# The last token group's closing sums: other banks, another order, one queue for the first output's stores

## The chip, the cores and the metric

The kernel runs on one NeuronCore of a Trainium2 chip. Its engines have queues of their own: TensorE (matmuls, and transposes by a matmul with the identity), VectorE and ScalarE (elementwise work, and the only ones that read what TensorE wrote to PSUM), GpSimd, and SyncE, which here only issues DMAs. ScalarE issues DMAs too. An engine takes its instructions in order; between engines, semaphores order the work. The metric is the device time of one execution in microseconds.

## The reference

A state-space block gives 3072 tokens of 256 features; they go through an expansion to 2048 features with a parametric ReLU, and back to 256. The change touches the end of the second product.

```
attn_out = _attn_ref(x, a, B, C)                  # (4, 8, 768, 32), scan in chunks
x = attn_out.transpose(0, 2, 1, 3).reshape(3072, 256)
h = x @ w_in                                      # (3072, 2048)
g = np.maximum(h, 0.0) + alpha * np.minimum(h, 0.0)
return (g @ w_out).astype(np.float32)             # (3072, 256)
```

## The kernel before

The tokens are worked on in six groups of 512 (`g`), the last being `g == NG - 1`. In each but the first, the 2048 hidden features are taken in four steps (`z`, called quads) of four blocks of 128. Both matrix products use a seven-product scheme in place of eight: the token half and the feature half of each operand are split in two, sums of them are formed on GpSimd and VectorE, and seven products are accumulated in PSUM. For the second product, `product(g, z, n)` (L1085) adds the share of quad `z` to sum number `n`. It is called for quad `z - 1` among the work of quad `z`, so that only the last quad's seven products are left for the end, in `close` (L1218).

A PSUM bank holds 512 numbers per partition, so two sums of 256 columns share one. `HALVES` and `LAST` (L1079, L1081) say for each sum the bank and the half of it; four banks are used, the fourth (`m5_bank`) for sum 5 and, in the last group, sum 4. In the last group sum 3 is computed turned, with tokens on the partitions, in two halves of 128 tokens (L1092 to L1100): its halves lie side by side in one half of bank 2. Before, sums 7 and 6 share bank 1. The framework tracks a bank as one tile: a matmul into it waits for an earlier read of any of its columns, and a read waits for the matmuls into it that were recorded before it.

`close` turns the seven sums into four 128 x 256 blocks of the output and stores them:

- `c[0][:, 0]` = sums 1 + 2, the first output. It is transposed in 32 x 32 blocks on VectorE in `turn` (L1276) and stored with four DMAs of 32 KB, in turn on SyncE and ScalarE.
- `c[0][:, 1]` = 6 + 1 + 5, to which 3 is added at the end. TensorE transposes it (`turned`, L1226), ScalarE copies it from PSUM to `rest`, and VectorE adds the halves of sum 3 to it (L1273). Each half has a store of its own.
- `c[1][:, 1]` = 7 + u + 5 and `c[1][:, 0]` = 7 + u - 4, where `u[:, 0]` = 6 + 1 and `u[:, 1]` = 7 + `u[:, 0]`. Both are transposed by TensorE, copied by ScalarE and stored with one 128 KB DMA each (`send`, L1232).

Just before `close`, `finish` stores the second output block of the group before (512 tokens, four DMAs of 64 KB on SyncE), so that these stores stand ahead of those of `close` in SyncE's queue. The order within each engine is the order of the calls in the source. Output buffers come from a pool of three (`op`).

Of the kernel before, what the change touches and what calls it, by code (L numbers as in the profile page):

```python
# [9 lines left out]
F32 = mybir.dt.float32  # L10
U32 = mybir.dt.uint32
U16 = mybir.dt.uint16
ALU = mybir.AluOpType
# [9 lines left out]
def kernel(  # L23
# [25 lines left out]
    nc = tc.nc  # L49
# [6 lines left out]
    P = 128  # L56
# [15 lines left out]
    NQ = NF // 2  # L72
    NZ = NF // 4
    HM = d_model // 2
    HT = GT // 2
# [13 lines left out]
    wtp = ctx.enter_context(tc.tile_pool(name="wtp", bufs=3))  # L89
# [8 lines left out]
    op = ctx.enter_context(tc.tile_pool(name="op", bufs=3))  # L98
    dr = ctx.enter_context(tc.tile_pool(name="dr", bufs=1, space=bass.MemoryType.DRAM))
    ps_s = ctx.enter_context(tc.tile_pool(name="ps_s", bufs=2, space=PSUM))  # L100
# [3 lines left out]
    def bank(i):  # L104


        return ps_q.tile([P, 512], F32, name="bank", tag=f"q{i}")
# [215 lines left out]
    def keep_warm(to, n, cols=2 * Q):  # L323

        for i in range(n):
# [8 lines left out]
                          in_=ident.unsqueeze(1).to_broadcast([P, H, Q]))  # L334
# [182 lines left out]
    def spare():  # L517

        return ps_h.tile([P, GT], F32, name="hp", tag="hp")
# [483 lines left out]
    def hidden_two(g, f, t0, hp):  # L1003


        nt = GT // 2
        ts = slice(t0, t0 + nt)
        for i in range(2):
            fs = slice((f + i) * P, (f + i + 1) * P)
            for k in range(KC):  # L1010
                nc.tensor.matmul(hp[:, i * nt : (i + 1) * nt], w_in[:, k, fs],  # L1011
                                 xts[g][:, k, ts], start=(i == 0 and k == 0),
                                 stop=(k == KC - 1), skip_group_check=True)
        for i in range(2):
            if t0 == 0:
                gts[g, f + i] = gp.tile([P, GT], F32, name="gt")
            nc.scalar.mul(gts[g, f + i][:, ts], hp[:, i * nt : (i + 1) * nt],
                          s_alpha[:, f + i : f + i + 1])

        def rest():  # L1020
            for i in range(2):
                gt = gts[g, f + i][:, ts]
                nc.vector.scalar_tensor_tensor(
                    out=gt, in0=hp[:, i * nt : (i + 1) * nt], scalar=s_mul[:, f + i : f + i + 1],
                    in1=gt, op0=ALU.mult, op1=ALU.max)
        return rest
# [51 lines left out]
    ms = {}  # L1078
    HALVES = {1: (0, 0), 2: (0, 1), 7: (1, 0), 6: (1, 1), 3: (2, 0), 4: (2, 1), 5: (3, 0)}  # L1079

    LAST = {**HALVES, 4: (3, 1)}  # L1081
    blocks = {}


    def product(g, z, n, parts=(0, 1), halves=(0, 1)):  # L1085

        if g not in ms:
            ms[g] = [t.rearrange("p (h t) -> p h t", h=2)
                     for t in [bank(i) for i in range(3)] + m5_bank]
        i, h = (LAST if g == NG - 1 else HALVES)[n]  # L1090
        s1, s2, s4 = out_sums
        if g == NG - 1 and n == 3:  # L1092
            for s in halves:
                ts = slice(s * P, (s + 1) * P)
                for p in parts:
                    q = 2 * z + p
                    nc.tensor.matmul(ms[g][i][:, h, ts], blocks[g, z][n][:, p, ts], s4[:, q],  # L1097
                                     start=(q == 0 and h == 0 and s == 0), stop=(q == NQ - 1),
                                     skip_group_check=True)
            return  # L1100
        for p in parts:
            q = 2 * z + p
            w = {1: wq[:, q, 0, 0], 2: wq[:, q, 1, 0], 3: s4[:, q], 4: wq[:, q, 1, 1],
                 5: s1[:, q], 6: s2[:, q], 7: wq[:, q, 0, 1]}[n]
            nc.tensor.matmul(ms[g][i][:, h], w, blocks[g, z][n][:, p],  # L1105
                             start=(q == 0 and h == 0), stop=(q == NQ - 1),
                             skip_group_check=True)
# [110 lines left out]
    def close(g):  # L1218

        m = {n: ms[g][i][:, h] for n, (i, h) in LAST.items()}  # L1220
        sa = wtp.tile([P, 2, HT], F32, name="sa", tag="wr")
        u = wtp.tile([P, 2, HT], F32, name="u", tag="wr")
        c = [one.tile([P, 2, HT], F32, name=f"c{i}") for i in range(2)]
        add = nc.vector.tensor_tensor

        def turned(t, ps):  # L1226

            for b in range(2):
                nc.tensor.transpose(ps[:, b * P : (b + 1) * P], t[:, b * P : (b + 1) * P], ident)
            return ps  # L1230

        def send(i, h, o, dma, bs=(0, 1)):  # L1232

            t0, n = g * GT + h * HT + bs[0] * P, len(bs)
            dma.dma_start(out=out[t0 : t0 + n * P, i * HM : (i + 1) * HM]
                          .rearrange("(b p) m -> p b m", p=P),
                          in_=o[:, bs[0] : bs[0] + n])

        def tokens():
            return op.tile([P, 2, HM], F32, name="o_sb")  # L1240

        for n in (1, 2):
            product(g, NZ - 1, n)
        nc.scalar.copy(out=sa[:, 0], in_=m[1])
        add(out=c[0][:, 0], in0=m[2], in1=sa[:, 0], op=ALU.add)
        turn(g, 0, c[0], slice(0, HT), [nc.sync, nc.scalar])
        product(g, NZ - 1, 6)
        add(out=u[:, 0], in0=m[6], in1=sa[:, 0], op=ALU.add)  # L1248
        product(g, NZ - 1, 5)
        nc.scalar.copy(out=sa[:, 1], in_=m[5])  # L1250
        add(out=c[0][:, 1], in0=u[:, 0], in1=sa[:, 1], op=ALU.add)
        product(g, NZ - 1, 7)
        add(out=u[:, 1], in0=m[7], in1=u[:, 0], op=ALU.add)
        add(out=c[1][:, 1], in0=u[:, 1], in1=sa[:, 1], op=ALU.add)
        ps = [ps_h.tile([P, 512], F32, name="turned", tag="hp") for i in range(2)]
        turned(c[0][:, 1], ps[0])
        rest = tokens()
        nc.scalar.copy(out=rest.rearrange("p b m -> p (b m)"), in_=ps[0][:, :HT])
        product(g, NZ - 1, 4)
        add(out=c[1][:, 0], in0=u[:, 1], in1=m[4], op=ALU.subtract)  # L1260
        turned(c[1][:, 1], ps[1])
        o = tokens()
        nc.scalar.copy(out=o.rearrange("p b m -> p (b m)"), in_=ps[1][:, :HT])
        send(1, 1, o, nc.sync)
        product(g, NZ - 1, 3, halves=(0,))
        ps = ps_s.tile([P, 512], F32, name="turned", tag="ss")
        turned(c[1][:, 0], ps)
        o = tokens()
        nc.scalar.copy(out=o.rearrange("p b m -> p (b m)"), in_=ps[:, :HT])
        send(1, 0, o, nc.scalar)  # L1270
        product(g, NZ - 1, 3, halves=(1,))
        for b in range(2):
            add(out=rest[:, b], in0=m[3][:, b * P : (b + 1) * P], in1=rest[:, b], op=ALU.add)  # L1273
            send(0, 1, rest, (nc.sync, nc.scalar)[b], (b,))

    def turn(g, i, c, ts, engs):  # L1276

        n = ts.stop - ts.start
        o = op.tile([P, GT], F32, name="o_sb")
        nc.vector.transpose(o[:, :n], c.rearrange("p h t -> p (h t)")[:, ts])  # L1280
        for a4 in range(P // 32):
            m0 = i * HM + 32 * a4
            t0 = g * GT + ts.start
            engs[a4 % len(engs)].dma_start(
                out=out[t0 : t0 + n, m0 : m0 + 32].rearrange("(b r) c -> r b c", r=32),
                in_=o[32 * a4 : 32 * a4 + 32, :n].rearrange("r (b c) -> r b c", c=32))
# [44 lines left out]
    rest = hidden_two(0, 2, 2 * Q, spare())  # L1331
# [61 lines left out]
    for i in range(NZ * (NG - 1)):  # L1393
        g, z = divmod(NZ + i, NZ)
# [39 lines left out]
        if i == 0:  # L1434
            load_pair(nxt + 1)
        quad(g, z, after, nxt >= NP or z % 2 == 0)
    close(NG - 1)


# [28 lines left out]
```

## Time and profile before

| What | us |
|---|---|
| median of four runs (lowest, highest) | 359.28 (359.07, 359.45) |
| the profiled execution: its time | 359.07 |
| its span, from first to last instruction | 357.4 |
| TensorE busy from 0 to 340 | 336.64 |
| TensorE busy from 340 to 350 | 9.83 |
| TensorE busy from 350 to the end | 3.57 |
| last matmul of the kernel starts | 353.66 |
| last store issued (ScalarE) | 354.55 |

The granted clock of TensorE is 1.0 throughout. The table's middle rows are from the busy time of each engine by stretches; the last two are single instructions of the trace.

A page or an answer of the trace is read like this: a row of the order of time gives the start, the length, the engine (PE is TensorE, PEld its weight loads, DVE VectorE, ACT ScalarE, POOL GpSimd, SP SyncE; a q behind the name stands for the sequencer that issues DMAs), the line of the kernel, the operation, the tile that is written and the tiles that are read, the size, and in brackets the idle time of that engine before it and what ended it. Each fp32 matmul of the source appears as two in the trace. Ends of matmuls are modelled, since they overlap.

### The profile page before, as it was taken

The page shows a single profiled execution, that of the slowest core. Times are in us where ns is not written, and L with a number is a line of the kernel's source. Part 1 is how long each engine was busy: PE and PEld are TensorE (multiplying, and loading weights), DVE is VectorE, ACT ScalarE, POOL GpSimd, SP SyncE. Part 2 cuts the span into 40 slices and gives each one's busy share as a digit, 9 for nine tenths or more (in the row PEclk, how much of TensorE's full clock was granted, in tenths as well). Part 3 has the DMA queues.
Part 4 walks back from the last instruction along what each step waited for, and adds up shares of the span by engine and source line. Part 5 has one row for each costly group of instructions (what it writes and reads, how often), then busy time and mean ns, then how long its engine had stood idle before and what let it go on. Part 6 is the DMA issues. An engine that isn't in the chain of part 4 may idle for free.

```text
span 357.4 us, 7565 instructions
## 1 busy us (share of the span) xinstructions
PE 350.0 (98%) x2894; PEld 287.6 (80%) x2894; DVE 240.4 (67%) x467; ACT 174.1 (49%) x387; POOL 205.6 (58%) x221
## 2 busy tenths in 40 slices
PE   8899999999999999999999999999999999999995
PEld 7576665578788888888888888888888888888884
DVE  7988986998748756857747847757856633653263
ACT  3677666535356346346345445345445344444331
POOL 4887568589939755725645725647626535533520
PEclk9999999999999999999999999999999999999999
DMA  7999999608245403403503413413001002002004
GB/s 112 195 188 324 292 224 234 137 17 181 84 91 125 95 2 76 103 2 85 99 26 79 89 45 74 88 48 73 2 4 29 0 2 31 0 0 32 0 3 88
DMA packets 105469, 30.19 MB, mean 84 GB/s; under 512 B 79880, under 2 KB 101336, under 8 KB 105432
## 3 DMA queue, kind: packets, MB, share of 16 engines
q1 hardware_dynamic: 104360, 29.39, 37.6%
q8 instruction: 23, 0.38, 0.4%
q10 hardware_dynamic: 1072, 0.31, 0.4%
q14 instruction: 14, 0.11, 0.1%
HBM read 26.32 MB, written 3.37 MB: 83 GB/s over the span
## 4 chain that ended last, share of the span: by engine, by line
PE 94%; POOL 1%; DMA 1%; ACT 1%; SPq 1%; issue 1%; DVE 1%; ACTq 0%; DVEq 0%; POOLq 0%
PE bank L1105 33%; PE hp L1130 28%; PE bank L1034 8%; PE hp L996 6%; PE ss L1130 6%; PE hp L1011 2%; PE ss L758 1%; PE ss L702 1%; PE bank L1097 1%; PE ss L750 1%; DMA nat<-in_C_dram 1%; PE ss L776 1%; PE ss L713 1%; PE bank L511 1%; PE ss L589 1%
## 5 line engine op out<-in xcount | busy, mean ns | idle before, releaser
L1187 POOL TENSOR_TENSOR gt<-gt 128x512 f32<-128x512 f32 x58 | 74.3, 1281 | 21.1 <-DVE gt L1115 16.2
L1105 PE MATMUL bank<-gt,w_out 128*128 128x256 f32 x320 | 83.8, 382 | 0.2 <-DVE u L1248 0.2
L1105 PEld LDWEIGHTS bank<-gt,w_out 128*128 128x128 f32 x320 | 60.0, 190 | 9.7 <-issue 1.6
L1115 DVE SCALAR_TENSOR_TENSOR gt<-hp,s_mul,gt 128x256 f32<-128x256 f32 x96 | 42.0, 479 | 29.1 <-ACT gt L1113 26.8
L1177 POOL TENSOR_TENSOR gt<-gt 128x512 f32<-128x512 f32 x20 | 25.4, 1271 | 62.5 <-DVE gt L1115 56.7
L1113 ACT ACTIVATE gt<-hp,s_alpha 128x256 f32<-128x256 f32 x96 | 40.4, 472 | 34.5 <-PE hp L1130 31.4
L1105 PE MATMUL bank<-gt,ws 128*128 128x256 f32 x224 | 55.9, 379 | 0.0
L1105 PEld LDWEIGHTS bank<-gt,ws 128*128 128x128 f32 x224 | 42.3, 190 | 5.6
L1130 PE MATMUL hp<-xs,w_in 128*128 128x256 f32 x160 | 41.9, 384 | 0.0
L1130 PE MATMUL hp<-xs,ws 128*128 128x256 f32 x160 | 41.2, 380 | 0.0
L1156 DVE TENSOR_TENSOR hp<-hp,u 128x512 f32<-128x512 f32 x20 | 14.0, 700 | 35.8 <-ACT u L1154 35.8
L1130 PEld LDWEIGHTS hp<-xs,ws 128*128 128x128 f32 x160 | 30.3, 190 | 4.3 <-POOL xs L1075 0.2
L1130 PEld LDWEIGHTS hp<-xs,w_in 128*128 128x128 f32 x160 | 29.7, 190 | 4.5
L1034 PE MATMUL bank<-w_out,gt 128*128 128x256 f32 x128 | 31.0, 384 | 0.0
L1034 PEld LDWEIGHTS bank<-w_out,gt 128*128 128x128 f32 x128 | 23.6, 190 | 6.5 <-issue 2.9
L1130 PE MATMUL ss<-xT,w_in 128*128 128x256 f32 x96 | 24.6, 379 | 0.0
L996 PE MATMUL hp<-xT,w_in 128*128 128x512 f32 x48 | 22.7, 596 | 0.1
L616 POOL TENSOR_TENSOR sm<-state,bmask 128x256 f32<-128x256 f32 (+1 forms) x10 | 6.2, 621 | 28.8 <-DVE state L613 28.8
L532 DVE TENSOR_TENSOR_SCAN dec<-abc,bank 128x192 f32<-128x192 f32 x48 | 22.7, 521 | 0.0
L1145 ACT COPY m<-hp 128x512 f32<-128x512 f32 x8 | 4.7, 587 | 35.7 <-PE hp L1130 35.7
L1154 ACT COPY u<-hp 128x512 f32<-128x512 f32 x20 | 11.7, 586 | 19.4 <-PE hp L1130 19.4
L1115 DVE SCALAR_TENSOR_TENSOR gt<-c,s_mul,gt 128x256 f32<-128x256 f32 x40 | 20.6, 555 | 0.0
(204 smaller groups left out, 617.3 us busy)
## 6 DMA issues: line engine op xcount, KB each, us to landing
abc<-z SPq DMA_DIRECT2D x24, 192.0 KB
raw<-in_moe_w_in_dram SPq DMA_DIRECT2D x8, 512.0 KB
raw<-in_moe_w_out_dram SPq DMA_DIRECT2D x8, 512.0 KB
abc<-z SPq DMA_DIRECT2D x8, 512.0 KB
out_dram<-o_sb SPq DMA_DIRECT2D x33, 64.0 KB
nat<-in_B_dram SPq DMA_DIRECT2D x26, 64.0 KB
nat<-in_C_dram SPq DMA_DIRECT2D x24, 64.0 KB
xt<-in_x_dram SPq DMA_DIRECT2D x12, 128.0 KB
```

What stands on the lines that cost most here:

```text
L532: nc.vector.tensor_tensor_scan(out=dv[:, o : o + SQ], data0=abc[k][:, s : s + SQ], data1=ident_p[0][:, :SQ], initial=0.0, op0=ALU.mult, op ...
L996: nc.tensor.matmul(hp, w_in[:, k, f * P : (f + 1) * P], xts[g][:, k], start=(k == 0), stop=(k == KC - 1))
L1011: nc.tensor.matmul(hp[:, i * nt : (i + 1) * nt], w_in[:, k, fs], xts[g][:, k, ts], start=(i == 0 and k == 0), stop=(k == KC - 1), skip_gro ...
L1034: nc.tensor.matmul(pos[0][t // 2][:, t % 2], gt[:, t * Q : (t + 1) * Q], w_out[:, f], start=(f == 0 and t % 2 == 0), stop=(f == NF - 1), s ...
L1105: nc.tensor.matmul(ms[g][i][:, h], w, blocks[g, z][n][:, p], start=(q == 0 and h == 0), stop=(q == NQ - 1), skip_group_check=True)
L1113: nc.scalar.mul(o[:, p], h[:, p], s_alpha[:, fs[p]])
L1115: nc.vector.scalar_tensor_tensor(out=o[:, p], in0=h[:, p], scalar=s_mul[:, fs[p]], in1=o[:, p], op0=ALU.mult, op1=ALU.max)
L1130: nc.tensor.matmul(to[:, p], w(2 * z + p), b, start=start and p == 0, stop=True, skip_group_check=True)
L1154: nc.scalar.copy(out=u2, in_=A)
L1156: nc.vector.tensor_tensor(out=Y, in0=Y, in1=u2, op=ALU.add)
L1177: nc.gpsimd.tensor_tensor(out=tc_, in0=g22, in1=g12, op=ALU.subtract)
L1187: eng.tensor_tensor(out=o, in0=x0, in1=x1, op=ALU.subtract)
```

## The change

Three things change, all in `product` and `close` for the last group:

- **Banks.** Sum 7 moves to the second half of bank 2. The two halves of sum 3 no longer lie side by side: the first is in the first half of bank 2 (128 columns), the second in the first half of bank 1 (`third_of`), where sum 7 was. So bank 1 holds sum 6 and the second half of sum 3, bank 2 sum 7 and the first half of sum 3.
- **Order.** TensorE takes the last quad's products as 1, 2, 6, 5, 7, 4, the transposes of `c[0][:, 1]`, the first half of 3, the transposes of `c[1][:, 1]` and of `c[1][:, 0]`, the second half of 3. Before, it was 1, 2, 6, 5, 7, the transposes of `c[0][:, 1]`, 4, those of `c[1][:, 1]`, the first half of 3, those of `c[1][:, 0]`, the second half. VectorE forms `u[:, 0]` ahead of the transpose of the first output, not behind it, and adds the first half of sum 3 on its own.
- **Stores.** All four stores of the first output are issued by SyncE (two by ScalarE before). Both halves of `rest` go out from SyncE too (the second from ScalarE before), the first of them now ahead of `c[1][:, 1]`. `c[1][:, 0]` stays on ScalarE. `rest` comes from another pool (`wtp`).

```diff
-    LAST = {**HALVES, 4: (3, 1)}
+    LAST = {**HALVES, 4: (3, 1), 7: (2, 1)}
+    def third_of(g, s):
+        return ms[g][2 - s][:, 0, :P]
...
-                    nc.tensor.matmul(ms[g][i][:, h, ts], blocks[g, z][n][:, p, ts], s4[:, q],
-                                     start=(q == 0 and h == 0 and s == 0), stop=(q == NQ - 1),
-                                     skip_group_check=True)
+                    nc.tensor.matmul(third_of(g, s), blocks[g, z][n][:, p, ts], s4[:, q],
+                                     start=q == 0, stop=(q == NQ - 1), skip_group_check=True)
...
+        def by_act(t, ps, o=None):
+            turned(t, ps)
+            o = tokens() if o is None else o
+            nc.scalar.copy(out=o.rearrange("p b m -> p (b m)"), in_=ps[:, :HT])
+            return o
...
-        turn(g, 0, c[0], slice(0, HT), [nc.sync, nc.scalar])
-        product(g, NZ - 1, 6)
+        for n in (6, 5):
+            product(g, NZ - 1, n)
         add(out=u[:, 0], in0=m[6], in1=sa[:, 0], op=ALU.add)
-        product(g, NZ - 1, 5)
         nc.scalar.copy(out=sa[:, 1], in_=m[5])
+        turn(g, 0, c[0], slice(0, HT), [nc.sync])
+        product(g, NZ - 1, 7)
         add(out=c[0][:, 1], in0=u[:, 0], in1=sa[:, 1], op=ALU.add)
-        product(g, NZ - 1, 7)
         add(out=u[:, 1], in0=m[7], in1=u[:, 0], op=ALU.add)
+        product(g, NZ - 1, 4)
         add(out=c[1][:, 1], in0=u[:, 1], in1=sa[:, 1], op=ALU.add)
+        add(out=c[1][:, 0], in0=u[:, 1], in1=m[4], op=ALU.subtract)
         ps = [ps_h.tile([P, 512], F32, name="turned", tag="hp") for i in range(2)]
-        turned(c[0][:, 1], ps[0])
-        rest = tokens()
-        nc.scalar.copy(out=rest.rearrange("p b m -> p (b m)"), in_=ps[0][:, :HT])
-        product(g, NZ - 1, 4)
-        add(out=c[1][:, 0], in0=u[:, 1], in1=m[4], op=ALU.subtract)
-        turned(c[1][:, 1], ps[1])
-        o = tokens()
-        nc.scalar.copy(out=o.rearrange("p b m -> p (b m)"), in_=ps[1][:, :HT])
-        send(1, 1, o, nc.sync)
+        rest = wtp.tile([P, 2, HT], F32, name="rest", tag="wt")[:, 0]
+        rest = by_act(c[0][:, 1], ps[0], rest.rearrange("p (b m) -> p b m", b=2))
         product(g, NZ - 1, 3, halves=(0,))
-        ps = ps_s.tile([P, 512], F32, name="turned", tag="ss")
-        turned(c[1][:, 0], ps)
-        o = tokens()
-        nc.scalar.copy(out=o.rearrange("p b m -> p (b m)"), in_=ps[:, :HT])
+        add(out=rest[:, 0], in0=third_of(g, 0), in1=rest[:, 0], op=ALU.add)
+        send(0, 1, rest, nc.sync, (0,))
+        send(1, 1, by_act(c[1][:, 1], ps[1]), nc.sync)
+        o = by_act(c[1][:, 0], ps_s.tile([P, 512], F32, name="turned", tag="ss"))
+        product(g, NZ - 1, 3, halves=(1,))
+        add(out=rest[:, 1], in0=third_of(g, 1), in1=rest[:, 1], op=ALU.add)
         send(1, 0, o, nc.scalar)
-        product(g, NZ - 1, 3, halves=(1,))
-        for b in range(2):
-            add(out=rest[:, b], in0=m[3][:, b * P : (b + 1) * P], in1=rest[:, b], op=ALU.add)
-            send(0, 1, rest, (nc.sync, nc.scalar)[b], (b,))
+        send(0, 1, rest, nc.sync, (1,))
```

## The prediction

> **What bounds it now.** First the page: busy shares and the chain say whether one engine carries the span. Then the order of time over the last ten microseconds, since only the close of the last token group is edited; then that stretch's waits and transfers.
>
> ```profile
> span 357.4 us, 7565 instructions
> ...
> PE 350.0 (98%) x2894; PEld 287.6 (80%) x2894; DVE 240.4 (67%) x467; ACT 174.1 (49%) x387; POOL 205.6 (58%) x221
> ...
> PE 94%; POOL 1%; DMA 1%; ACT 1%; SPq 1%; issue 1%; DVE 1%; ACTq 0%; DVEq 0%; POOLq 0%
> ```
>
> TensorE is the bound for 347 us, and nothing there changes in amount: the built order shows the same matmuls before and after. What can change is the close, where TensorE waits. Columns: start, length (merged where several), engine, line, what, and in brackets the idle time before and its releaser.
>
> ```profile
> 348.86 0.45 DVE L1280 STREAM_TRANSPOSE o_sb<-c 128x256 f32<-128x256 f32 x1
> 349.23 0.38 DVE L1248 TENSOR_TENSOR u<-bank,sa 128x256 f32<-128x256 f32 x1
> 349.34 0.96 ACTq L1284 DMA_DIRECT2D out_dram<-o_sb  x2
> ...
> 349.76 1.10 PE L1105 MATMUL bank<-gt,w_out 128*128 128x256 f32 x4 [0.17 <-DVE u L1248]
> 350.35 0.37 ACT L1250 COPY sa<-bank 128x256 f32<-128x256 f32 x1 [2.08 <-DVE u L1248]
> 350.75 0.42 DVE L1251 TENSOR_TENSOR c<-u,sa 128x256 f32<-128x256 f32 x1 [1.14 <-ACT sa L1250]
> 351.09 0.42 DVE L1253 TENSOR_TENSOR u<-bank,u 128x256 f32<-128x256 f32 x1
> ...
> 351.23 0.44 PE L1229 MATMUL turned<-ident,c 128*128 128x128 f32 x2 [0.37 <-DVE c L1251]
> ...
> 353.33 0.61 PE L1097 MATMUL bank<-ws,gt 128*128 128x128 f32 x4
> 353.53 0.37 ACT L1269 COPY o_sb<-turned 128x256 f32<-128x256 f32 x1 [0.36 <-PE turned L1229]
> 353.93 0.98 ACTq L1235 DMA_DIRECT2D out_dram<-o_sb  x2
> 354.03 0.49 DVE L1273 TENSOR_TENSOR o_sb<-bank,o_sb 128x128 f32<-128x128 f32 x2 [1.03 <-PE bank L1097]
> ```
>
> Three things stand here. Product 7 starts at 349.76 though TensorE was free at 349.43: it shares a bank with product 6, and waits until VectorE has read that (L1248), which itself stands behind a transpose. ScalarE issues two stores (349.34 to 350.31) and only then copies product 5, which was complete at 349.59; so the sum L1251 and the transpose by TensorE come late: TensorE is idle from 350.63 to 351.23. Last, both final adds wait for the whole of product 3. Behind the last store, issued at 354.55, come its landing (completion events at 356.26) and 1.1 us of closing waits.
>
> **Part by part.** Steps, from the rows: a product of two fp32 128x256 matmuls holds TensorE 0.865 (four passes of 0.216) and ends 0.16 later; a half of product 3 0.45; a pair of transposes 0.22; a ScalarE copy 0.37 and a VectorE add 0.42, each released some 0.04 after its source; overlapping VectorE instructions start 0.34 after the one before.
>
> *Product 7 to product 3's bank.* That bank has no reader yet, so the wait falls: product 7 at 349.43 to 350.30, **-0.33**. Product 3 half 0 now waits in turn for the reading of product 7 (u[:,1]), but that ends at 350.92 and half 0 stands at 351.39: hidden, 0.47 to spare. Earlier quads gain no wait in the built order.
>
> *Stores of the first output from SyncE.* ScalarE copies product 5 at 349.63, ends 350.00 (before: 350.72). VectorE: c0[:,0] 348.30, then u[:,0] 348.78 to 349.16, the transpose 349.12 to 349.57, c0[:,1] 350.04 to 350.46, u[:,1] when product 7 is out, 350.50 to 350.92, c1[:,1] 350.96 to 351.38, c1[:,0] when product 4 is out (351.32), 351.36 to 351.78.
>
> *Product 4 ahead of the transposes.* It needs the copy of product 5 (350.00): 350.30 to 351.17, no wait. Transposes of c0 351.17, half 0 351.39 to 351.84 (out 352.00), transposes of c1[:,1] 351.84, of c1[:,0] 352.06 (its add ended 351.78), half 1 352.28 to 352.73, out 352.89. Before, it was out at 353.94, so TensorE ends **1.05 earlier**: 0.33 and 0.60 of waits, and 0.12 of restarts around transposes that came late.
>
> *Halves of product 3 in two banks.* The first add no longer waits for half 1: 352.09 to 352.38. The second takes 352.93 to 353.21, against 354.52: another 0.26.
>
> *Stores.* SyncE: first half of `rest` at 352.41, the 128 KB of c1[:,1] at 352.83 (it is copied by 352.63, and now stands behind the other), second half at 353.27, against 354.55 from ScalarE before: **-1.28**. ScalarE copies c1[:,0] 352.67 to 353.04 and issues it at 353.07, against 353.93: -0.86. `rest` in another pool costs nothing; it even leaves out a wait for old stores.
>
> *What SyncE pays.* Ahead of these it now has eight turned stores instead of six. The fourth of the previous 512-token output ends at 349.60; the next two took 0.63 and 0.50 with 0.05 between. Two more at 0.50 to 0.63 make SyncE free at 352.0 to 352.3, against 352.41: hidden with 0.1 to 0.4 to spare. Here a rule speaks against the change: the Trainium skill, "DMA: Bandwidth & Descriptors", section Issuing engines are not separate DMA queues, says all issuing engines share the 16 DMA engines and a second issuer saves only sequencer time, which the edit gives up. The row agrees on the price, about 1.1 us of SyncE; but on ScalarE the same 0.96 held the path. By the rule alone the sum is up to 1.1 worse, by the rows 0. I take the rows.
>
> *The drain.* How fast do the last stores move?
>
> ```profile
> DMA packets 560, 0.26 MB, mean 238 GB/s; under 512 B 48, under 2 KB 560, under 8 KB 560
> ...
> q10 hardware_dynamic: 416, 0.20, 60.2%
> q1 hardware_dynamic: 144, 0.07, 19.6%
> ```
>
> This is 354.8 to 355.9: all 16 engines together give 238 GB/s with both ramps, about 290 in the full slices. Before, four stores were issued over 1.36 us and each landed 1.68 to 1.89 after its issue, hardly delayed. Now the last three, 320 KB, are issued within 0.44. With no queueing they land at 353.27 + 1.71 = 354.98 and 353.07 + 1.89 = 354.96, 1.28 ahead of 356.26. With queueing: first packet 0.88 after 352.83, at 353.71; 328 kB at 290 GB/s 1.13, at 250 1.31; 0.37 from last packet to completion: 355.21 to 355.39, 1.05 to 0.87 ahead. The same page's Specifications give 435 GB/s for the fabric: by that 0.75, no queueing and the full 1.28; the row, with its 512-byte packets, says otherwise, and I take **1.0**, nearer to it. The closing waits stay at 1.1: the number after the last second-half store is the same.
>
> **Sum.** 357.35 - 1.0 = 356.35 of span. The profiled execution took 359.07, so 358.07; it was the fastest of four whose median is 359.28, so for a median I expect 359.28 - 1.0 = **358.3**.
>
> **Rivals.**
> 1. *The drain eats more.* If the four stores queue behind the turned ones (384 KB in 128-byte packets, 107 GB/s from 350 to 352), or TensorE's order costs 0.2 to 0.3 in handovers of 0.04 that I placed too tightly, 0.4 to 0.7 is left: 358.6 to 358.9. For it: eight turned stores on one queue, first in first out. Against: on one queue alone they already ran full from 348.3 to 349.9, and the last is issued 0.4 before the first of the final stores.
> 2. *SyncE becomes the bound, and it is slower.* One of the 34 turned stores on SyncE took 1.71 instead of 0.5 (at 322.1), and the second in the close 0.79. Everything but c1[:,0] stands behind the turned stores. Last issue before: 354.55. Two issues of 0.42 stand ahead of the last, so the change turns to a loss when SyncE is free later than 353.7, that is when its last four turned stores take over 0.98 each on average. One stall of 1.2 leaves 0.2 to 0.5 of gain (358.8 to 359.1); descriptors that come at 1.3 each, as under the loads of the first 60 us where issues took over 2, give free at 355.1, last issue 356.0, 1.4 late: 360.7. Against: no load runs in the close, and this line's median is 0.50.
> 3. *The wait is only moved.* If product 3 half 0 waited for more than the reading of product 7, or product 4 for a later copy, TensorE would idle again by up to 0.6: gain 0.4, 358.9. Against: the built order names only u[:,1] and the copy of product 5.
>
> **Numbers.** Forecast 0.62. Rival 1 0.14 and rival 3 0.06, of which most ends within 0.2% (0.72 us, about what a measurement tells from no change); rival 2 with one stall 0.08, with a loss 0.10. A forecast at 0.75 still counts as faster, and some of rival 1 too: faster 0.66, same 0.23, slower 0.11. Range 357.7 (no queueing, and c1[:,0] the last to land, which shortens the closing waits by up to 0.26) to 359.2 (one stall in SyncE): outside are the loss and some extremes. For the forecast alone: 357.9 to 358.5.
>
> **What would show it.** Product 7 without a wait at about 349.4; the copy of product 5 at 349.6; TensorE without a gap from product 1 to its end near 352.9; first add while half 1 runs; SyncE's last turned store issued before 352.4; last issue near 353.3; completion near 355.2. It is wrong if SyncE is still issuing turned stores when the first add is done, or if a store completes over 2.1 after its issue.

## The result, and the profile after

| | median us (lowest to highest) | runs |
|---|---|---|
| before | 359.20 (358.78 to 360.40) | 61 |
| after | 358.77 (358.20 to 360.96) | 41 |

The ratio is 0.9989, with a 95% interval of 0.9984 to 0.9995, which is 0.2 to 0.6 us: **0.43 us less** by the medians. The gain is clear of the noise, but it stays under the 0.2% (0.72 us) that the prediction wanted for "faster". It lies in the range, on the side that was forecast, at less than half the forecast of 1.0.

The profiled execution of the changed kernel took 358.54. Its page:

```profile
span 356.8 us, 7561 instructions
...
PE 350.6 (98%) x2894; PEld 288.8 (81%) x2894; DVE 239.1 (67%) x467; ACT 174.1 (49%) x387; POOL 205.0 (57%) x221
...
PE 86%; SPq 7%; DVE 3%; DMA 1%; POOL 1%; ACT 1%; issue 1%; DVEq 0%; ACTq 0%
```

The span is 0.6 shorter at the same number of matmuls. The 7% of SPq in the chain are loads at the start (the chain there runs through SyncE in one execution and through TensorE in another); in the close it differs from before. There, the chain of work that ended last ran over ScalarE's second store, its copy of product 5 and a VectorE add to TensorE; now it is TensorE's without a break to the last add. Pieces of that chain (start, length, what) from before, then from after:

```profile
349.72 0.58 ACTq L1284
...
350.35 0.38 ACT sa L1250
...
350.75 0.44 DVE c L1251
```

```profile
345.80 5.83 PE bank L1108 x27
351.63 0.22 PE turned L1232 x2
```

The order of time in the close (columns as before):

```profile
349.08 0.42 DVE L1258 TENSOR_TENSOR u<-bank,sa 128x256 f32<-128x256 f32 x1
349.42 0.43 DVE L1284 STREAM_TRANSPOSE o_sb<-c 128x256 f32<-128x256 f32 x1
...
349.74 1.89 PE L1108 MATMUL bank<-gt,w_out 128*128 128x256 f32 x8
349.94 0.37 ACT L1259 COPY sa<-bank 128x256 f32<-128x256 f32 x1 [1.35 <-PE bank L1108]
350.34 0.42 DVE L1262 TENSOR_TENSOR c<-u,sa 128x256 f32<-128x256 f32 x1 [0.49 <-ACT sa L1259]
...
351.53 0.45 SPq L1288 DMA_DIRECT2D out_dram<-o_sb  x1
...
352.40 0.29 DVE L1271 TENSOR_TENSOR rest<-bank,rest 128x128 f32<-128x128 f32 x1 [0.31 <-PE bank L1101]
...
352.57 0.61 PE L1101 MATMUL bank<-ws,gt 128*128 128x128 f32 x4
352.72 0.36 SPq L1238 DMA_DIRECT2D out_dram<-rest  x1
353.18 0.39 SPq L1238 DMA_DIRECT2D out_dram<-o_sb  x1
353.21 0.29 DVE L1276 TENSOR_TENSOR rest<-bank,rest 128x128 f32<-128x128 f32 x1 [0.52 <-PE bank L1101]
353.23 0.44 ACTq L1238 DMA_DIRECT2D out_dram<-o_sb  x1
353.66 0.42 SPq L1238 DMA_DIRECT2D out_dram<-rest  x1
```

Product 7, in the row of 349.74 together with product 4, has no bracket: TensorE no longer waits for it, nor anywhere else. ScalarE copies product 5 as soon as it is out, the first add (352.40) no longer waits for the second half of product 3 (352.57), and the last store is the second half of `rest`.

These rows can't be laid beside the old ones by their clock. In every trace of any version, what comes before the close takes up to 1.1 us more or less, and this arises in the first 48 us. So each close is measured from one event that the change leaves alone, the start of the 128 x 512 transpose on VectorE in the `finish` ahead of it (called T below: 346.64 before, 346.96 after):

| us after T | before | after |
|---|---|---|
| last matmul starts | 7.02 | 5.95 |
| last store issued | 7.91 | 6.70 |
| last landing | 9.62 | 8.77 |
| end of the span | 10.71 | 9.88 |

TensorE ends 1.07 earlier, the last issue is 1.21 earlier, the last landing 0.85. The close before does not always take 10.71. In its four traces in this order (two of them with an edit far ahead of the close) ScalarE's second store is issued by 3.66, 3.61, 3.56 and 3.45 after T, and each time the last matmul starts 3.35 to 3.36 after that; the close takes 10.71, 10.65, 10.62 and 10.49. This is the path that the prediction named, seen at work.

Where do the last 0.36 go, and why do the medians show 0.43 when this pair of closes shows 0.83? The drain, from 353.9 to 355.5:

```profile
DMA packets 692, 0.33 MB, mean 206 GB/s; under 512 B 50, under 2 KB 692, under 8 KB 692
...
q1 hardware_dynamic: 420, 0.20, 42.0%
q10 hardware_dynamic: 272, 0.13, 26.5%
```

Three stores, 0.33 MB, move in one stretch, where 0.26 MB moved before, and the last lands 2.1 after its issue (353.66 to 355.73, where the kernel before had 1.71). That is the first answer. For the second, the experiments show a part.

### The profile page after: what moved, and what is told of

It reads as the page before. It is cut to its first block, busy times and chain, and to the rows that moved or that the text cites. A ratio compares the mean times of both kernels' runs of the same rounds, so it can differ in the third digit from the quotient of the medians.

```text
span 356.8 us, 7561 instructions
## 1 busy us (share of the span) xinstructions
PE 350.6 (98%) x2894; PEld 288.8 (81%) x2894; DVE 239.1 (67%) x467; ACT 174.1 (49%) x387; POOL 205.0 (57%) x221
## 4 chain that ended last, share of the span: by engine, by line
PE 86%; SPq 7%; DVE 3%; DMA 1%; POOL 1%; ACT 1%; issue 1%; DVEq 0%; ACTq 0%
PE bank L1108 33%; PE hp L1133 29%; PE bank L1034 6%; PE ss L1133 6%; PE hp L996 3%; SPq L188 3%; SPq L192 2%; DMA raw<-in_moe_w_in_dram 1%; PE ss L758 1%; DVE dec L538 1%; PE ss L702 1%; PE bank L1101 1%; PE ss L750 1%; PE ss L776 1%; DVE wr L296 1%
```

## The experiments

The theory at the start: the gain on the engines is whole, and the drain eats part of it. The rivals: SyncE, with eight turned stores ahead of the final ones, is late in some executions; or one part of the change costs what another brings. All runs, each with the kernel before beside it on the same chip (the ratio with its interval is an estimate over all runs of both, and not the quotient of the two medians):

| run | median us (runs) | before beside it | ratio (95%) | last landing after T |
|---|---|---|---|---|
| before, again | 359.66 (20) | 359.37 | 1.0000 (0.9991 to 1.0009) | 9.57 |
| after, again | 358.98 (22) | 359.37 | 0.9988 (0.9978 to 0.9998) | 9.28 |
| after, stores on two queues | 358.59 (8) | 359.37 | 0.9966 (0.9953 to 0.9980) | 8.76 |
| before, stores from SyncE only | 360.11 (22) | 359.37 | 1.0014 (1.0002 to 1.0026) | 10.44 |
| after, 20 matmuls more at the start | 365.93 (6) | 359.24 | 1.0183 (1.0155 to 1.0211) | 8.75 |
| before, the same | 367.10 (6) | 359.24 | 1.0218 (1.0180 to 1.0256) | 9.53 |
| after, `rest` in the output pool | 359.53 (20) | 359.24 | 1.0011 (1.0002 to 1.0021) | 9.93 |
| before, stores from SyncE, `rest` apart | 358.80 (12) | 359.24 | 0.9989 (0.9979 to 0.9999) | 9.08 |
| after, fetch moved | 358.69 (21) | 359.18 | 0.9993 (0.9983 to 1.0003) | 8.77 |
| after, banks undone | 358.48 (21) | 359.18 | 0.9985 (0.9974 to 0.9996) | 8.91 |
| before, fetch moved | 359.35 (21) | 359.18 | 1.0011 (1.0002 to 1.0019) | 9.40 |
| two queues, fetch moved, `c[1][:, 1]` early | 358.40 (22) | 359.18 | 0.9979 (0.9971 to 0.9987) | 8.49 |

### Both kernels again

No edit: a second trace of each.

> The kernel before, unedited: its spread and a second trace of it. The traces differ by +0.31 us before 45 us and by -0.88 from the first store of the close to the end, but the medians by only -0.43. Theory A (the gain in the close varies): the close, from SyncE's first store after 347 us to the end of the span, took 9.98 before and repeats within 0.1, and the start of the close repeats to a few tenths either way. Theory B (the changed kernel starts later in every run): start of the close within 0.1 of 347.37. Theory C (the start draws freely, no other cause): start of the close anywhere within 0.4, ratio 1.000.

> The changed kernel, unedited. Theory A: close between 9.1 and 9.7 in this trace, not 9.13 again, ratio near 0.9989. Theory B: close 9.1 again, and its start near 347.65 again, ratio near 0.9989. Theory C: close 9.1 again, start anywhere within 0.4 of 347.4, ratio near 0.9976.

Before repeats itself (landing 9.57 against 9.62). After does not: 9.28 against 8.77, with the same last matmul (5.94). SyncE and VectorE in the second trace of the changed kernel:

```profile
351.36 1.90 SPq L1288 DMA_DIRECT2D out_dram<-o_sb  x1
...
352.18 0.29 DVE L1271 TENSOR_TENSOR rest<-bank,rest 128x128 f32<-128x128 f32 x1 [0.31 <-PE bank L1101]
...
353.36 0.40 SPq L1238 DMA_DIRECT2D out_dram<-rest  x1
353.85 0.39 SPq L1238 DMA_DIRECT2D out_dram<-o_sb  x1
354.33 0.44 SPq L1238 DMA_DIRECT2D out_dram<-rest  x1
```

The eighth turned store holds SyncE for 1.90, where the others took 0.45. The first half of `rest` is added by 352.47 and would be stored from 352.5, but its issue stands at 353.36, and the two behind it follow in steps of 0.49: the last is at 354.33, though its data was there at 353.29. This is the rival of the late SyncE, with one stall. What else ran when it began? The transfers from 351.3 to 351.5 of the same trace:

```profile
q1 hardware_dynamic: 142, 0.02, 59.1%
q8 instruction: 1, 0.02, 46.7%
```

A packet of 16 KB of instructions starts at 351.36, with the blocked issue. By its count, queue q8 carries TensorE's own program: 23 such packets stand in the page of the changed kernel, one per some 250 of its 5788 matmuls and weight loads, and added TensorE instructions shift them, as the next runs show. Each packet takes 0.88 to 2.1 in that trace, and the last falls into the close.

### Taking the fetch out of the close

If the fetch makes the stall, a kernel in which it falls elsewhere has none. The first attempt shifts it by 20 unused matmuls at the start (both kernels):

```diff
-    keep_warm(ps_h.tile([P, GT], F32, name="hp"), WARM, Q)
+    hp0 = ps_h.tile([P, GT], F32, name="hp")
+    keep_warm(hp0, WARM, Q)
+    keep_warm(hp0, 20, 8)
```

> The changed kernel with 20 small matmuls more (128 x 8, result unused) at its start, which put 80 TensorE instructions in front of everything and so the last 16 KB instruction fetch of TensorE some 80 instructions, about 8 us, earlier: near 343 and not at 351.4 to 352.2 amid the turned stores. Theory (a fetch holds one of the 16 DMA engines, turned stores queue there, and a SyncE issue that meets it blocks, 1.90 in the second trace of the changed kernel): no SyncE issue of the close over 0.9, all turned stores landed within 0.3 of each other by 353, last landing about 8.6 to 8.8 after the start of the transpose of 512 columns, and against its control (the kernel before with the same matmuls) -0.8 to -1.0 us with a narrow spread. Rival (the drain itself queues, whatever the fetch): still 8.8 to 9.3, and -0.3 to -0.6 against the control. The start of the kernel may be up to 2 us longer in both.

> Control: the kernel before with the same 20 small matmuls at its start. Its fetch at 352.2 fell into a pause of the transfers (351.7 to 354.0), so moving it changes nothing in the close: last landing 9.55 to 9.65 after the transpose of 512 columns, as in both traces of the kernel before. What its time differs from the kernel before is the price of the matmuls at the start (0 to 2 us).

As timings both failed: the kernels took 7 to 8 us more, spent in the start; what of it the shifted fetches cost wasn't looked into. But the closes can be read: no fetch in them, no long issue, and landings at 8.75 and 9.53.

The second attempt adds the instructions late: in quad 1 of the last group the matmuls of the first product, 256 columns wide, are made as two of 128.

```diff
+            n = 2 if (g, z) == (NG - 1, 1) else 1
...
-                nc.tensor.matmul(to[:, p], w(2 * z + p), b, start=start and p == 0, stop=True,
-                                 skip_group_check=True)
+                for c in range(n):
+                    cs = slice(c * HT // n, (c + 1) * HT // n)
+                    nc.tensor.matmul(to[:, p, cs], w(2 * z + p), b[:, cs],
+                                     start=start and p == 0 and c == 0, stop=True,
+                                     skip_group_check=True)
```

> The changed kernel, with the 14 expansion matmuls of quad 1 of the last group taken in halves of 128 columns (28 in place of 14, the same work): 56 TensorE instructions more, so that the last instruction fetch of TensorE falls some 6 us earlier, near 345.5 to 346.5, before any store of the close; the start of the kernel is untouched, unlike with the small matmuls there. Cost of the halves: four passes of 0.216 become eight of 0.11, so at most 0.3 in all. Theory (fetch meets the turned stores and a SyncE issue): no SyncE issue of the close over 0.9, last landing 8.7 to 8.9 after the transpose of 512 columns, ratio to before 0.9973 to 0.9980, narrow spread. Rival (the drain's queueing alone halves the gain): ratio 0.9986 to 0.9990 as for the changed kernel.

> Control: the kernel before with the same 14 matmuls in halves. Its fetch met no store, so the close stays at 9.55 to 9.65 to the last landing; time 359.1 to 359.6, the difference to before being the price of the halves (0 to 0.3).

Transfers from 351 to 354, of the changed kernel and then of the one with the fetch moved (GB/s in 40 equal slices of that stretch, then the queues):

```profile
GB/s 92 121 135 91 16 0 17 90 128 120 52 3 0 48 119 345 96 21 0 12 79 142 113 60 5 0 0 7 7 7 7 9 9 10 84 256 309 185 62 7
q1 hardware_dynamic: 1248, 0.20, 38.3%
q8 instruction: 1, 0.02, 1.8%
```

```profile
GB/s 127 91 138 137 91 17 0 22 97 135 128 52 3 0 49 126 143 100 19 0 17 87 142 130 57 5 0 0 0 0 0 0 0 0 0 96 280 301 171 28
q1 hardware_dynamic: 1343, 0.21, 40.1%
```

The fetch is gone (it lies 10 us earlier), and each turned store of the first output takes 0.45. Between these two kernels the close is 0.61 shorter after the change (9.88 against 10.49), and the medians differ by 0.66 (358.69 against 359.35). The median of before with the edit is 0.17 above before; in the traces the halved matmuls cost 0.21.

Two things expected here did not come. The changed kernel with the fetch moved was to be at 0.9973 to 0.9980 of before; it is at 0.9993, no faster than the changed kernel without that edit. And the control was to land at 9.55 to 9.65; it landed at 9.40, by its earlier stores on ScalarE. So only the difference between the two speaks for the fetch, and the runs don't separate its 0.66 (95%: 0.34 to 0.86) from the 0.43 (0.30 to 0.66) without the edit. What the blocked issue costs the median is thus not shown. And a close without a stall proves little by itself, since some with the fetch have none either. The stronger sign is in what follows.

A control for this lies in the trace already. At 322, in the previous `finish`, the prediction had noted one issue of 1.71 and taken it for a rare draw. SyncE before the change from 321.7 to 324.5, then transfers of that trace from 322.05 to 322.3:

```profile
321.74 3.15 SPq L1284 DMA_DIRECT2D out_dram<-o_sb  x4
```

```profile
q8 instruction: 1, 0.02, 30.9%
```

and SyncE of before with the fetch moved:

```profile
322.34 1.95 SPq L1288 DMA_DIRECT2D out_dram<-o_sb  x4
```

Four stores take 3.15 with a fetch at the second one's start, and 1.95 without. In eight of the nine traces that have the fetch there, that second store took 1.38 to 1.81; in the ninth the fetch came 0.26 before the third store, and that one took 1.31. In the five in which the fetch is moved, each took 0.51 at most. So it was no rare draw. In the close the eighth turned store of SyncE starts at T + 4.5 to 4.6. In six traces with eight such stores and the fetch in place, the fetch came at T + 4.56 and 4.62 in two, and these were blocked (1.73 and 1.90); in the other four, including the first trace of the changed kernel, it came at T + 4.82 to 5.45, and nothing was blocked. Over all fourteen traces, from 64 us on, 28 issues on SyncE start within 0.1 of a fetch: all ten that store the output took 1.38 to 1.90, of the eighteen others seven took 1.30 to 1.79 and eleven 0.48 to 0.64. What in the DMA path blocks an issue isn't shown, nor why some of the others escape; that these stores are blocked with the fetch, and not without it, is.

### Stores alone, and where `rest` lives

Only the first output's stores are moved to SyncE, in the kernel before:

```diff
-        turn(g, 0, c[0], slice(0, HT), [nc.sync, nc.scalar])
+        turn(g, 0, c[0], slice(0, HT), [nc.sync])
```

> The kernel before, with only one part of the change: the four stores of the first output from SyncE. By the prediction's steps the copy of product 5 comes 0.72 earlier, and the transposes behind product 7 start at 350.63 instead of 351.23; the waits of product 7 (0.33) and of both final adds for all of product 3 stay. So -0.6 at most on TensorE, ratio 0.9983 to 0.9988. If the stores are only shifted to another wait: 0.9995 to 1.0005.

This is slower than before, by 0.14% and outside both forecasts, though TensorE ends 0.5 sooner. The rows:

```profile
354.70 0.37 ACT L1269 COPY o_sb<-turned 128x256 f32<-128x256 f32 x1 [1.78 <-DMA out_dram<-o_sb]
355.10 0.94 ACTq L1235 DMA_DIRECT2D out_dram<-o_sb  x2
```

ScalarE's last copy waits 1.78 for a store. With three output buffers, the fifth block (that of `finish` counted as the first) needs the second one's buffer, which the four turned stores of the first output hold. They were issued by 351.79, but one of the 16 DMA engines finished its part of the last two some 1.6 to 1.9 us after the others (at 354.40 and 354.60). In the first trace of the changed kernel, stores 2, 3 and 4 landed on 15 engines by 352.20, 352.69 and 353.18, on the last at 354.28, 354.50 and 354.72. This is the trickle of 7 to 10 GB/s in the first of the two rows of GB/s above; here too the transfers from 353.2 to 353.6 are a trickle, of 4 to 11. With the fetch moved, it is gone and all 16 are within 0.3. That the late engine is the one with the fetch follows from this; the trace doesn't number the engines.

The change keeps `rest` in another pool, so its last copy needs an older buffer. Two kernels take that edit apart: the changed one with `rest` back among the outputs, and stores from SyncE with `rest` apart.

```diff
-        rest = wtp.tile([P, 2, HT], F32, name="rest", tag="wt")[:, 0]
+        rest = op.tile([P, 2, HM], F32, name="o_sb").rearrange("p b m -> p (b m)")
```

```diff
-        turn(g, 0, c[0], slice(0, HT), [nc.sync, nc.scalar])
+        turn(g, 0, c[0], slice(0, HT), [nc.sync])
...
-        rest = tokens()
+        rest = wtp.tile([P, 2, HT], F32, name="rest", tag="wt")[:, 0].rearrange("p (b m) -> p b m", b=2)
```

> The changed kernel with one part undone: rest comes from the pool of the output tiles again. Then the ScalarE copy of c1[:,0] waits until all four turned stores of the first output have landed, because it takes their buffer. They landed as late as 354.5 to 354.7 (one engine of 16). Theory (buffer wait): that copy starts near 354.3 instead of 352.8, the last store is issued 1.0 or more later, and the time is 0.8 to 1.5 above the changed kernel's, slower than before. The prediction's step (the pool costs nothing): within 0.1 of the changed kernel.

> The kernel before with the four stores of the first output on SyncE (as in the run with the stores alone, which was slower at 360.1) and rest in the other pool. Theory (buffer wait): the ScalarE copy of c1[:,0] no longer waits for the turned stores, and the loss turns into a gain: 358.7 to 359.1, with SyncE issues of up to 1.9 in part of the executions. If the loss came from eight issues on SyncE, it stays at 359.8 to 360.3.

The changed kernel with `rest` among the outputs, then stores from SyncE with `rest` apart, both in the order of time:

```profile
351.74 1.73 SPq L1288 DMA_DIRECT2D out_dram<-o_sb  x1
...
354.77 0.37 ACT L1249 COPY o_sb<-turned 128x256 f32<-128x256 f32 x1 [1.69 <-DMA out_dram<-o_sb]
355.18 0.41 ACTq L1238 DMA_DIRECT2D out_dram<-o_sb  x1
```

```profile
352.96 0.37 ACT L1269 COPY o_sb<-turned 128x256 f32<-128x256 f32 x1 [0.29 <-PE turned L1229]
...
353.99 0.36 ACTq L1235 DMA_DIRECT2D out_dram<-rest  x1
```

In the first, the eighth turned store is blocked until 353.47 and the copy waits until the four stores of that buffer have landed. The median is 0.29 above before: the pool alone is worth 0.22% (0.9989 against 1.0011, some 0.8 us), and without it the change is slower than before. In the second, the copy waits only for TensorE, and 1.0014 becomes 0.9989. As far as twelve runs can tell, these two edits alone bring what the whole change brings, though TensorE's last matmul starts at T + 6.49 here and not at 5.95: the other half of TensorE's gain, from order and banks, shows no worth in the time.

### Banks

The banks as before, all else changed:

```diff
-    LAST = {**HALVES, 4: (3, 1), 7: (2, 1)}
+    LAST = {**HALVES, 4: (3, 1)}
...
-        return ms[g][2 - s][:, 0, :P]
+        return ms[g][2][:, 0, s * P : (s + 1) * P]
...
-                                     start=q == 0, stop=(q == NQ - 1), skip_group_check=True)
+                                     start=q == 0 and s == 0, stop=(q == NQ - 1), skip_group_check=True)
```

> The changed kernel with the banks of before: sum 7 beside sum 6, both halves of sum 3 side by side; order and stores as changed. The prediction's step (the bank takes 0.33 of wait from product 7): TensorE ends 0.3 to 0.45 later. Rival (the order on VectorE took that wait away, since u[:,0] is read by 349.2 now, before product 7's turn at 349.43; the banks only let half 1 of product 3 run beside the first add): product 7 without a gap, half 1 waits some 0.1 to 0.2 for the first add, last matmul 6.1 after the transpose of 512 columns and not 5.95; time within 0.2 of the changed kernel.

```profile
349.40 1.89 PE L1108 MATMUL bank<-gt,w_out 128*128 128x256 f32 x8
...
352.40 0.52 PEld L1101 LDWEIGHTS bank<-ws,gt 128*128 128x128 f32 x4 [0.25 <-DVE rest L1271]
352.41 0.71 PE L1101 MATMUL bank<-ws,gt 128*128 128x128 f32 x4
```

In this order of time, product 7 (349.40, with product 4) starts without a wait though it shares the bank with product 6 again. The new order, in which `u[:, 0]` reads product 6 ahead of the transpose, is enough to free it; whether the bank alone would have been isn't tried. What the banks do bring is at the end: the second half of product 3 waits for the first add, and the last matmul starts at T + 6.23, not 5.95. The time shows no loss from that (358.48, 0.9985), so with the new order the banks are worth nothing that can be measured.

### Two queues, and a version with three edits

The changed kernel with the stores on two queues, which now stand behind the copy of product 5:

```diff
-        turn(g, 0, c[0], slice(0, HT), [nc.sync])
+        turn(g, 0, c[0], slice(0, HT), [nc.sync, nc.scalar])
```

> The changed kernel, with the four stores of the first output on SyncE and ScalarE in turn again; they stand behind the copy of product 5 on ScalarE, so that this copy stays early. If eight stores in a row on SyncE cost anything (theory A with the turned stores as its cause): SyncE is free at 351 instead of 352, the turned stores land by 352.5 and not as late as 354.7, the last store lands under 1.9 after its issue instead of 2.12, and the time is 0.1 to 0.3 below the changed kernel's. If they cost nothing (the prediction's step): within 0.1 of it. If ScalarE's copies are held up by its stores: first copy of the close's transposes later than 1.57 idle, time 0.1 to 0.4 above.

The last landing is that of an undisturbed changed kernel (8.76), but not in the way that was expected: two turned stores were late on one engine here as well (354.16 and 354.34, a fetch came at 351.78), and the last store landed 2.06 after its issue, not under 1.9. So in the changed kernel the turned stores, on one queue or two, late or not, don't move the last landing as long as SyncE isn't blocked; this speaks against the prediction's first rival, in which the final stores queue behind them. The ratio of 0.9966 rests on eight runs, too few to weigh it against the others.

The last kernel takes the two queues and the moved fetch, and puts the 128 KB of `c[1][:, 1]` ahead of the first half of product 3, so that a large store starts sooner:

```diff
         rest = by_act(c[0][:, 1], ps[0], rest.rearrange("p (b m) -> p b m", b=2))
+        send(1, 1, by_act(c[1][:, 1], ps[1]), nc.sync)
         product(g, NZ - 1, 3, halves=(0,))
...
-        send(1, 1, by_act(c[1][:, 1], ps[1]), nc.sync)
```

> A candidate: the changed kernel with the fetch moved as above, the turned stores of the first output on two queues, and the transposes and the 128 KB store of c1[:,1] ahead of the first half of product 3. By the rows the first 128 KB are issued 0.8 earlier and 384 KB drain from 353.3 on and not 320 KB from 353.7: last landing 8.4 to 8.6 after the transpose of 512 columns, 358.0 to 358.3. If the drain is not what the end waits for: 8.7 to 8.8 as in the run with two queues.

```profile
352.23 0.71 PE L1236 MATMUL turned<-ident,c 128*128 128x128 f32 x4
...
353.38 0.39 SPq L1242 DMA_DIRECT2D out_dram<-o_sb  x1
...
353.87 0.90 SPq L1242 DMA_DIRECT2D out_dram<-rest  x2
354.05 0.40 ACTq L1242 DMA_DIRECT2D out_dram<-o_sb  x1
```

In this order of time TensorE still ends at T + 6.06 (5.95 in the changed kernel), the last issue is at about T + 6.7 as there, and the last landing comes 0.28 sooner (8.49): the large store on SyncE is now ahead of both small ones. At 0.9979 it is 0.78 under before and 0.29 under the changed kernel with the fetch moved, both beside it on one chip; its 358.40 is just above the 358.0 to 358.3 that were expected. It is not shown to beat the changed kernel: the one with the banks undone had 358.48 on that chip, and the two intervals overlap. Which of the three edits brings what isn't taken apart.

## Why the prediction was right, and where its sizes were not

The range held, but that says little: its upper end of 359.2 is the time before. The prediction gave 0.66 to a gain over 0.2% and 0.23 to a change within 0.2%, and the latter came. What was right is the path.

- **TensorE ends 1.05 earlier**: it was 1.07. Right in sum, but the 0.33 of product 7 was put to the bank. With the new order on VectorE the bank isn't needed for it, as the prediction's own times say (product 6 read by 349.16, product 7 due at 349.43); the bank gives the end of product 3 instead.
- **Stores off ScalarE**: right. The copy of product 5 starts 0.20 after product 7, as worked out (349.63 against 349.43), and the brackets of 0.17 and 0.37 before product 7 and the transposes are gone.
- **Last issue 1.28 earlier**: 1.21. The second add ended 1.34 earlier, 1.31 was forecast.
- **What SyncE pays**: this is the term that was furthest off, by its cost of 0. Its arithmetic held where nothing interfered (eight stores end at T + 5.0, and the first half of `rest` is ready at T + 5.7), but in two of six traces the eighth was blocked for 1.3 to 1.45 more. In the one of these two that is the changed kernel the landing came 0.51 later (9.28 against 8.77), and SyncE was still issuing the eighth when the first add was done (353.26 against 352.47), which the prediction had named as a sign of being wrong. The second rival, with one stall of 1.2 that leaves 0.2 to 0.5 of the gain, describes the second trace: 0.33 of gain in the close (10.38 against 10.71). It was given 0.08, beside the remark that one issue in 34 was long. The question to ask was what else happened at 322.1; the queue of instructions had the answer, in the trace of before. The loss of up to 1.1 that was set against the rows did not come.
- **`rest` in another pool costs nothing**: right in sign, but its note on a wait left out was not followed to a price. That wait is worth some 0.8 us, twice the result.
- **The drain, 1.0 of 1.28**: 0.85 of 1.21 in the best case. The queueing was worked out as 0.87 to 1.05, and the value taken lay towards the end of no queueing; the trace lies just below the other end. The other sign of being wrong came too: a store that completes over 2.1 after its issue. The last took 2.07, but the 128 KB on ScalarE took 2.28 (353.23 to 355.51) and the first half of `rest` 2.20. The estimate of 0.75 for these 320 KB, by the 435 GB/s of the Trainium skill ("DMA: Bandwidth & Descriptors", Specifications), is not what the rows show: packets of 512 bytes moved at 206 GB/s with both ramps (238 in the close of before).

The mechanism was thus right, and two terms of its sum were mis-sized: 0.15 in the drain, and up to 0.5 in SyncE in part of the executions. What is left can be the spread of the closes. Against the mean of the four closes before (10.62), an undisturbed close after (9.88) gains 0.74 and the one with the stall (10.38) 0.24; half the executions with it and half without would give about 0.5, which lies within the interval of the result (0.2 to 0.6). This fits the 0.43, but it is an estimate from single traces: how often the timed runs have the stall isn't seen, and that it makes up what is missing isn't shown.

## What to carry to other kernels

A long issue in a queue is not a random draw until the other queues of the same microsecond have been looked at; TensorE's own instruction fetches move with the number of its instructions (56 more put the last one 10 us earlier). So one can see in the trace of before which stores they may meet, to within the 0.9 us over which the last one varied in the six traces. When stores move to another queue, follow the buffers that they hold as well as the engines: who takes that buffer next, and when does the slowest of the 16 DMA engines let it go? And gains of an engine in the close are not gains of the end: work the last landings out as one stream of bytes. (That the largest store should go first is only suggested here, by one trace.)

## What was not expected of the hardware

- A store issued on SyncE within 0.1 us of a 16 KB instruction fetch took 1.4 to 1.9 instead of 0.45 to 0.5, ten times out of ten. Not every issue near a fetch is long: of the eighteen that aren't stores of the output, eleven took 0.48 to 0.64 (a load at 143.17 in the first trace of the changed kernel 0.54). Nor does every long issue have a fetch: one at about 85 us took 1.2 to 2.5 in eleven traces, with no fetch within 6 us. What sets these apart was not tried.
- With a fetch of 0.89 us in flight, one DMA engine was 1.5 to 2.1 late with the 128-byte packets of three stores, more than the fetch's own length.
- What comes before the close differs by up to 1.1 us between traces, of one kernel too (346.96 and 346.74 for the changed one; 346.6 to 347.7 over all with the usual start), and it arises in the first 48 us. With changes of half a microsecond at the end, the close has to be measured from an event of its own.
